# Block 0's V projection: the turned tokens held in TensorE, the weights streamed in 512 columns, and V turned by DMA before its store

## The chip, the cores and the metric

The kernel runs on one core of a Trainium2 chip. The metric is the device time of one execution in microseconds. Three runs of the kernel before gave 1614.95, 1615.28 and 1615.65 us; the median is 1615.28 us. The profile shows one more execution: it took 1615.54 us, and its span, from its first to its last profiled instruction, is 1613.7 us.

## The reference

The input is 2048 tokens of 1024 values in bf16. Two pairs of layers follow each other; each pair is an attention layer and a gated layer, both with a layer norm before and a residual sum behind:

```python
x = A_x
x = x + _A_ref(_layernorm(x, axis=-1), A_wqkv, A_wo)
x = x + _B_ref(_layernorm(x, axis=-1), B_W_gate, B_W_up, B_W_down)
x = x + _A_ref(_layernorm(x, axis=-1), A_wqkv, A_wo)
x = x + _B_ref(_layernorm(x, axis=-1), B_W_gate, B_W_up, B_W_down)
```

`_A_ref` multiplies by `wqkv` (1024 x 3072) and splits the result into q, k and v of 32 heads with 32 values each. A token attends to eight earlier tokens at distances 0, 2, ..., 14; the weighted sum of their v goes through `wo` (1024 x 1024). `_B_ref` computes `relu(x @ W_gate) * (x @ W_up)` with 3584 columns and multiplies by `W_down`.

## The kernel before, in words

The tokens are cut into four blocks of 512 (`BLK`), a block into four tiles of 128 tokens (`TPB`). With two layer pairs there are eight rounds `n`; `n` 0 to 3 are the four blocks of the first pair. All of the change lies in the attention of `n = 0`, in the first 110 us.

A projection needs the normalised tokens with the 1024 channels on the partitions. `xn` holds tokens on partitions, `xnT` holds the turned form, eight chunks `kc` of 128 channels. For blocks 1 to 3 `xn` is turned by a DMA (`turn` in `ln_steps`, L291): tile by tile in block 1, in one transfer of 1 MB in blocks 2 and 3. Block 0 is written by hand in `ln_first` (L327) and `v_first` (L483): tiles 0 to 2 are turned on TensorE (`tp`) and copied back, tile 3 by DMA (`turn_last`). Tiles 0 and 1 are turned before their factor 1/std is known. So `spread_rstd` (L399) lays the factors of these 256 tokens out along the free axis on all partitions (`rb`: four VectorE transposes and six GpSimd copies), and `widen` (L411) multiplies `xnT` of both tiles by it in place, which q and k need.

V of block 0 is needed with channels on partitions, because the scratch tensor `v_d` in HBM is stored channel by channel. The kernel before holds a 128 x 128 piece of the weights in TensorE and streams turned tokens: 192 products of 128 columns and 32 of 256 columns (`prod` in `v_first`). The result in PSUM is V turned already. VectorE evicts tiles 0 and 1 with the factor `rb` (`scaled`), ScalarE evicts tiles 2 and 3. `store_v(0)` writes the whole `vT` to `v_d` in one transfer, and `load_v_steps(0)` reads it back as `vhm`, one transfer per tile, with a halo of 14 tokens.

After V of block 0, TensorE computes q and k of block 0, then q and k of block 1, V of blocks 1, 2 and 3, then q and k of blocks 2 and 3, with eight products of 512 columns per 128 output columns (1.73 us, `GRP`). PSUM gives six banks for these results (tag `acc`). q and k of block 1 are evicted by ScalarE into staging tiles (`qst`, `kst`; pool `stage`, six buffers in a ring) and put to HBM by SyncE's queue (`put`); so `kst` number 7 gets the buffer of `kst` number 1 and has to wait until that one is stored.

What sets the order of the work:

- `ev` is a list of (time, step). It is sorted by the time written there, and the steps are emitted in that order (`emit`).
- TensorE, VectorE and SyncE's DMA queue run in exactly the emitted order: `mm` (L141), `dv` (L115) and `sp_dma` (L130) tie each instruction to the one before it. All DMAs named here go through SyncE's queue, which waits at its head.
- ScalarE and GpSimd are tied only in places (`tail_act`, `last`). Elsewhere the framework's scheduler chooses the order when the program is built, by its own estimate of when each operand is ready. That order is fixed in the program: at run time ScalarE takes its instructions strictly one after the other.
- A buffer that is reused brings a wait for the last reader of what was in it; the pool `early` has three such buffers for `xn` and `vT`.

Of the kernel before, what the change touches and what calls it, by code (L numbers as in the profile page):

```python
# [8 lines left out]
F32 = mybir.dt.float32  # L9
ALU = mybir.AluOpType  # L10
# [3 lines left out]
P = 128  # L14
# [5 lines left out]
HALO = (W - 1) * DIL  # L20
KC = D // P
BLK = 512
TPB = BLK // P
EPS = 1e-5
NEG = -1.0e9
SLAB = 512
# [5 lines left out]
def _ap(t, off, dims):  # L32
    return bass.AP(tensor=t.tensor, offset=t.offset + off, ap=[list(t.ap[0])] + [list(d) for d in dims])
# [3 lines left out]
def kernel(  # L37
# [11 lines left out]
    nc = tc.nc  # L49
# [31 lines left out]
    psum = ctx.enter_context(tc.tile_pool(name="psum", bufs=6, space=bass.MemoryType.PSUM))  # L81
# [28 lines left out]
    def dv(f, *args, **kwargs):  # L110
        if tail_dve[0] is None:
            tail_dve[0] = f(*args, **kwargs).ins
        else:
            with tc.issue_after(tail_dve[0]):
                tail_dve[0] = f(*args, **kwargs).ins  # L115
# [8 lines left out]
    def sp_dma(dst, src, transpose=False):  # L124
        start = nc.sync.dma_start_transpose if transpose else nc.sync.dma_start
        if tail_sp[0] is None:
            tail_sp[0] = start(dst, src).ins
        else:
            with tc.issue_after(tail_sp[0]):
                tail_sp[0] = start(dst, src).ins  # L130

    @contextmanager
    def pe_group():
        if tail_pe[0] is None:
            yield
        else:
            with tc.issue_after(tail_pe[0]):
                yield

    def mm(*args, **kwargs):  # L140
        tail_pe[0] = nc.tensor.matmul(*args, **kwargs).ins  # L141

    def big_tile(shape, name, early=False):
        where = pool["early"] if early else big
        return where.tile(shape, BF16, tag="big", name=name)
# [47 lines left out]
    slab = {}  # L193
# [133 lines left out]
    def ln_first():  # L327
# [4 lines left out]
        def on(eng, f, *args, **kwargs):  # L332
            if eng == "v":
                dv(f, *args, **kwargs)
            elif eng in last:
                with tc.issue_after(last[eng]):
                    last[eng] = f(*args, **kwargs).ins
            else:
                last[eng] = f(*args, **kwargs).ins
# [19 lines left out]
        def power(t, var, sign, eng="g"):  # L359
            vpe = small("vpe1")  # L360
            rstd[t] = pair[:, t:t + 1] if t < 2 else small("rstd1")[:]
            if eng == "v":
                on("v", nc.vector.tensor_scalar, vpe[:], var, EPS, None, op0=ALU.add)
            else:
                on("g", nc.gpsimd.tensor_scalar, vpe[:], var, sign, EPS, op0=ALU.mult, op1=ALU.add)
            on("g", nc.gpsimd.tensor_tensor, rstd[t], vpe[:], neg_half[:, 0:1], op=ALU.pow)
# [27 lines left out]
        def act_power(t, sq):  # L394
            nvar = small("nvar1")
            on("v", nc.vector.scalar_tensor_tensor, nvar[:], mean[t], mean[t], sq[:], op0=ALU.mult, op1=ALU.subtract)
            power(t, nvar[:], -1.0)

        def spread_rstd():  # L399
            rb = hold["rb"] = pool["early"].tile([P, 2, P], F32, tag="rb", name="rb", bufs=1)  # L400
# [41 lines left out]
        def open_up():  # L442
# [5 lines left out]
            for h in range(4):  # L448
# [5 lines left out]
            power(0, square_of(xna[:, 0, :])[:], 1.0)  # L454

        hold.update(on=on, bn=bn, aggr=aggr, apply=apply, turn=turn, copy=copy, widen=widen,
                    spread_rstd=spread_rstd, open_up=open_up, last=last, square_of=square_of, act_mean=act_mean,
                    act_power=act_power)
        return hold

# [21 lines left out]

    def v_first(ln):  # L483
        st = att[0]
        pairs, opened = {}, set()

        def prod(kc, c, t0, t1):
            part = t0 // 2
            if (part, c // 2) not in pairs:
                pairs[part, c // 2] = psum.tile([P, 2, BLK // 2], F32, tag="acc", name="acc_v")  # L490
            acc = pairs[part, c // 2][:, c % 2, (t0 % 2) * P:(t0 % 2 + t1 - t0) * P]
            with pe_group():
                mm(acc, lhsT=slab["v0", kc // (KC // 2)][:, kc % (KC // 2), c * P:(c + 1) * P],
                   rhs=ln["xnT"][:, t0:t1, kc, :], start=(part, c // 2) not in opened, stop=(kc == KC - 1),
                   skip_group_check=True)
            opened.add((part, c // 2))

        def scaled(i):
            dv(nc.vector.tensor_tensor, st["vT"][:, 2 * i:2 * i + 2, 0:2 * P], pairs[0, i][:],
               _ap(ln["rb"], 0, [[0, 2], [1, 2 * P]]), op=ALU.mult)  # L500

        def later(t, h):
            ln["turn"](t, (h,))
            ln["copy"](t, "a", h, 2 - h)

        def turn_last():
            sp_dma(ln["xnT"][:, TPB - 1, :, :], ln["xn"][:, TPB - 1, :], True)
            load_x(1, [1])

        def halves(i, part, k0):  # L510
            for c in (2 * i, 2 * i + 1):
                for kc in range(k0, KC):
                    prod(kc, c, 2 * part, 2 * part + 2)

        def head():
            st["vT"] = big_tile([P, KC, BLK], "vT_0", True)
            ln["open_up"]()

            def chunk(kc, t):
                for c in range(KC):  # L520
                    prod(kc, c, t, t + 1)

            for kc in range(3):
                chunk(kc, 0)
            ln["turn"](1, (0,))
            ln["copy"](1, "v", 0)
            ln["turn"](1, (1,))
            ln["copy"](1, "a", 1)
            chunk(3, 0)
            ln["spread_rstd"]()  # L530
            for kc in range(4):
                chunk(kc, 1)
            for c in range(KC):
                prod(4, c, 0, 2)
            ln["bn"](2, 0)
            ln["bn"](2, 1)
            ln["aggr"](2)
            sq = ln["square_of"](x_tiles[3][:])
            ln["act_mean"](3)
            ln["act_power"](3, sq)  # L540
            ln["apply"](2)
            ln["apply"](3)
            turn_last()
            for c in range(KC):
                prod(5, c, 0, 2)
            for c in range(4):
                prod(6, c, 0, 2)
            for i in range(KC // 2):
                if i == 3:
                    later(2, 0)  # L550
                halves(i, 0, 7 if i < 2 else 6)
                if i == 3:
                    later(2, 1)
                scaled(i)
            ln["widen"]()
            q = KC // 4
            for cs, kcs in ((range(0, 2 * q), range(0, q)), (range(0, 2 * q), range(q, 2 * q)),
                            (range(2 * q, 3 * q), range(0, 2 * q)), (range(0, 2 * q), range(2 * q, KC)),
                            (range(3 * q, KC), range(0, 2 * q)), (range(2 * q, KC), range(2 * q, KC))):
                for c in cs:  # L560
                    for kc in kcs:
                        prod(kc, c, 2, 3)
            for c in range(KC):
                for kc in range(KC):
                    prod(kc, c, 3, 4)
                if c % 2 == 1:
                    ln["on"]("a", nc.scalar.copy, st["vT"][:, c - 1:c + 1, 2 * P:BLK], pairs[1, c // 2][:])
            tail_act[0] = ln["last"]["a"]

        return head  # L570

    def store_v(n):
        def f():
            dst = bass.AP(tensor=v_d.tensor, offset=v_d.offset + HALO + (n % NB) * BLK,
                          ap=[[NTOK, P], [P * NTOK, KC], [1, BLK]])
            sp_dma(dst, att[n]["vT"][:])
        return f
# [202 lines left out]
    def load_v_steps(n):  # L780
        b = n % NB

        def f_(tq):
            def f():
                if tq == 0:
                    att[n]["v_hm"] = soft.tile([P, DH, HALO + P], BF16, tag="v_hm", name=f"vhm_{n}")
                src = bass.AP(tensor=v_d.tensor, offset=v_d.offset + b * BLK + tq * P,
                              ap=[[DH * NTOK, H], [NTOK, DH], [1, HALO + P]])
                sp_dma(att[n]["v_hm"][32 * tq:32 * tq + 32, :, :], src)
            return f  # L790

        return [f_(tq) for tq in range(TPB)]
# [188 lines left out]
    def spread(steps, at, gap):  # L981
        for i, f in enumerate(steps):
            ev.append((at + gap * i, f))
# [54 lines left out]
               (t_sum0 - 0.1, t_sum0 + 4.5, t_sum0 + 4.6), (t_qk0 + 10.6, t_qk0 + 15.8, t_qk0 + 15.9)]  # L1038
    for t, steps in enumerate(norm_at):
        ev.extend(zip(steps, (stats[t], apply[t], turn(t))))  # L1040
    ev.append((t_qk0 + 4.0, store_v(0)))
    ev.append((t_qk0 + 18.0, lambda: load_x(3)))
    spread(qk_steps(0, ln_a[0], "qk01"), t_qk0, GRP)
    spread(prod_sum_steps(0), t_sum0, 4.4)
    spread(load_v_steps(0), t_qk0 + 19.0, 1.0)
    ln1(2, t_qk0 + 17.5, t_qk1 + 17.0, True, 4.5)
    qk1, puts1, gets1 = (part[0::2] + part[1::2] for part in qk_steps(1, ln_a[1], "qk01", True))
    spread(qk1, t_qk1, GRP)
# [142 lines left out]
```

## Time and profile before

| what | value |
|---|---|
| median of the runs | 1615.28 us (1614.95 to 1615.65) |
| the profiled execution, its span | 1615.54 us, 1613.7 us |
| TensorE busy | 1606.9 us, all 40 slices at 9 tenths or more, granted clock 1.00 |
| waits of TensorE in the whole span | 1.1 us and 0.4 us, both before 7.5 us |
| VectorE, ScalarE, GpSimd busy | 1139.4, 477.5, 186.7 us |
| V of block 0 on TensorE | 5.8 to 21.8 us, 224 products and 16 turns |
| V of blocks 1 to 3 on TensorE | 76.9 to 119.0 us |
| ScalarE busy from 42 to 76 us | nearly all of it |

Times in the views are microseconds from the start of the span. A busy TensorE is not by itself TensorE at its peak, since ends of products are modelled; how many products run in a stretch says more. A row of the timeline gives start, duration, engine, line, operation, tiles, shape and count; neighbours of the same kind are merged into one row. Durations of SyncE's rows are the time that issuing takes; the time to landing stands in the DMA view.

### The profile page before, as it was taken

Reading aid. Unit: us, or ns where it says so; the run is one execution under the profiler, and the core shown is the slowest. Engines: PE = TensorE matmul, PEld = TensorE weight load, DVE = VectorE, ACT = ScalarE, POOL = GpSimd, SP = SyncE. Lnnn points to the kernel's source line nnn. Section 1 sums busy time; section 2 is a strip of 40 time slices with the busy share of each in tenths; the row PEclk is TensorE's granted clock in tenths of the full one; section 3 lists DMA queues with packets and bytes.
Section 4 is the critical chain, followed back from the end, with each engine's and each line's share of the span. In section 5 each row is a group of like instructions: output and inputs, shape, how many; then the busy total and the mean of one; then the engine's idle time right before and its main releaser. Section 6 shows DMA issues by size and latency. Waiting matters only on the chain.

```text
span 1613.7 us, 18950 instructions
## 1 busy us (share of the span) xinstructions
PE 1606.9 (100%) x7604; PEld 785.4 (49%) x7653; DVE 1139.4 (71%) x963; ACT 477.5 (30%) x978; POOL 186.7 (12%) x173
## 2 busy tenths in 40 slices
PE   9999999999999999999999999999999999999999
PEld 7646544444444445444454444544445444444444
DVE  6999978997989698929389393993939939311211
ACT  4953311131115313603136031361313311131110
POOL 3400000010003002300053000530005100000000
PEclk9999999999999999999999999999999999999999
DMA  9977867596669666784747857488574874655452
GB/s 285 201 202 251 211 173 244 185 227 203 200 199 230 190 187 200 202 244 147 228 154 206 233 158 227 155 197 257 164 227 155 207 241 157 209 160 179 157 165 71
DMA packets 360473, 318.20 MB, mean 197 GB/s; under 512 B 106304, under 2 KB 334656, under 8 KB 359872
## 3 DMA queue, kind: packets, MB, share of 16 engines
q1 hardware_dynamic: 359808, 316.36, 67.1%
q8 instruction: 60, 0.98, 0.3%
q10 hardware_dynamic: 576, 0.62, 0.1%
q14 instruction: 29, 0.24, 0.1%
HBM read 266.29 MB, written 34.66 MB: 186 GB/s over the span
## 4 chain that ended last, share of the span: by engine, by line
PE 86%; DVE 10%; DMA 2%; issue 1%; ACT 0%; SPq 0%; POOL 0%; DVEq 0%; ACTq 0%; POOLq 0%
PE acc_u L141 21%; PE acc_g L141 21%; PE dacc L141 17%; PE acc_v L141 6%; PE dacc_pair L141 6%; PE acc_wo L141 5%; PE acc_q L141 5%; PE acc_k L141 5%; DVE pv L115 4%; DVE ac L115 2%; DVE t L115 2%; DMA s<-s_d 1%; DVE hT L115 1%; DVE x L115 0%; DMA xnT_b<-xn_b 0%
## 5 line engine op out<-in xcount | busy, mean ns | idle before, releaser
L141 PE MATMUL acc_g<-xnT_b,w_g 128*128 128x512 bf16 x1792 | 423.3, 379 | 0.0
L141 PE MATMUL acc_u<-xnT_b,w_u 128*128 128x512 bf16 x1792 | 423.3, 379 | 0.0
L891 ACT ACTIVATE r<-acc_g 128x512 bf16<-128x512 f32 x224 | 133.6, 596 | 721.2 <-PE acc_g L141 678.0
L115 DVE TENSOR_TENSOR hT<-acc_u,r 128x512 bf16<-128x512 f32 x224 | 150.8, 686 | 240.2 <-PE acc_u L141 237.6
L141 PE MATMUL dacc<-w_d,hT 128*128 128x512 bf16 (+1 forms) x1372 | 301.9, 376 | 1.5
L141 PEld LDWEIGHTS <-hT 128*128 128x128 bf16 x1820 | 177.0, 98 | 210.2
L141 PEld LDWEIGHTS <-w_u 128*128 128x128 bf16 x1792 | 175.4, 98 | 211.4
L141 PEld LDWEIGHTS <-w_g 128*128 128x128 bf16 x1792 | 175.3, 98 | 211.4
L115 DVE TENSOR_TENSOR pv<-a,vhm 128x4096 bf16<-128x4096 bf16 x64 | 143.5, 2283 | 0.0
L943 DVE TENSOR_TENSOR x<-dacc,x 128x512 bf16<-128x512 f32 (+1 forms) x38 | 24.7, 676 | 154.0 <-PE dacc L141 154.0
L704 DVE TENSOR_TENSOR t<-q,k 128x2048 f32<-128x2048 bf16 x56 | 128.0, 2292 | 6.7 <-ACT k L640 4.6
L115 DVE TENSOR_TENSOR t<-q,k 128x2048 f32<-128x2048 bf16 x56 | 127.3, 2284 | 0.9
L645 POOL COPY kh<-k 128x14 bf16<-128x14 bf16 x40 | 58.4, 1467 | 497.9 <-ACT k L640 497.9
L115 DVE TENSOR_TENSOR pv<-pv 128x1024 bf16<-128x1024 bf16 (+1 forms) x128 | 113.7, 949 | 0.0
L141 PE MATMUL acc_wo<-w_o,oT 128*128 128x512 bf16 x498 | 111.1, 379 | 0.7
L720 DVE TENSOR_TENSOR ac<-ac,t 128x2048 f32<-128x2048 f32 x48 | 109.7, 2285 | 0.3
L115 DVE TENSOR_TENSOR ac<-ac,t 128x2048 f32<-128x2048 f32 x48 | 109.6, 2283 | 0.0
L274 POOL TENSOR_TENSOR st_b<-st_b,neg_half 128x1 f32<-128x1 f32 x29 | 45.8, 1586 | 526.4 <-ACT st_b L273 521.6
L141 PE MATMUL dacc_pair<-w_d,hT 128*128 128x512 bf16 (+1 forms) x413 | 94.0, 375 | 0.4
L141 PEld LDWEIGHTS <-oT 128*128 128x128 bf16 x512 | 50.1, 98 | 60.4
L269 ACT ACTIVATE xn_b<-x 128x1024 bf16<-128x1024 bf16 x29 | 30.3, 1045 | 132.8 <-DVE x L115 70.6
L478 ACT CAST vT<-acc_v 128x512 bf16<-128x512 f32 x56 | 32.5, 585 | 54.3 <-PE acc_v L141 53.3
(142 smaller groups left out, 1235.3 us busy)
## 6 DMA issues: line engine op xcount, KB each, us to landing
w_g<-in_B_W_gate_dram SPq DMA_DIRECT2D x56, 1024.0 KB, 7.1
w_u<-in_B_W_up_dram SPq DMA_DIRECT2D x56, 1024.0 KB, 5.3
w_d<-in_B_W_down_dram SPq DMA_DIRECT2D x48, 1024.0 KB, 5.8
w_o<-in_A_wo_dram SPq DMA_DIRECT2D x16, 1024.0 KB, 8.3
vhm<-v_d SPq DMA_DIRECT2D x32, 284.0 KB, 6.8
v_d<-vT SPq DMA_DIRECT2D x8, 1024.0 KB, 9.5
oT<-o_d SPq DMA_DIRECT2D x32, 256.0 KB, 3.6
w_d<-in_B_W_down_dram SPq DMA_DIRECT2D x16, 512.0 KB, 3.6
```

What stands on the lines that cost most here:

```text
L115: tail_dve[0] = f(*args, **kwargs).ins
L141: tail_pe[0] = nc.tensor.matmul(*args, **kwargs).ins
L269: nc.scalar.activation(xn, xt[:], ACT.Square, accum_out=sq)
L274: nc.gpsimd.tensor_tensor(rstd, vpe, neg_half[:, 0:1], op=ALU.pow)
L478: tail_act[0] = nc.scalar.copy(st["vT"][:, c, :], acc[:]).ins
L645: nc.gpsimd.tensor_copy(khalo[n][:, c, :], k[:, BLK:BLK + HALO])
L704: nc.vector.tensor_tensor(t[:], i0, i1, op=ALU.mult)
L720: nc.vector.tensor_tensor(o, i0, i1, op=ALU.add)
L891: tail_act[0] = nc.scalar.activation(rs[j][:], acc[:], ACT.Relu).ins
L943: run = dv if n < NB - 2 else (lambda f, *args, **kwargs: f(*args, **kwargs))
```

## The change

Block 0's V is computed the other way round: a 128 x 128 piece of the turned tokens is held, and 512 columns of the weights stream past it. That makes 64 products instead of 224, and V comes out with tokens on partitions. It is evicted into `xn` of block 0, whose contents are no longer needed: tiles 0 and 1 by VectorE with the factor 1/std as a value per partition (`rpair`), tiles 2 and 3 by ScalarE (`put` in `v_first`). `spread_rstd` is called later, the small steps around tile 3's factor are ordered differently, and one of them goes from GpSimd to VectorE.

Because V is now not turned, four DMA turns on SyncE's queue (`turn_v`) bring it into `vT` after block 3's tokens have been requested. Five transfers store it to `v_d` (`store_v_first`), written at times between the puts of block 1's q. `load_v_steps(0)` moves from `t_qk0 + 19.0` to `t_qk1 + 17.1`, just behind the turn of block 2.

```diff
-        def act_power(t, sq): ...  power(t, nvar[:], -1.0)
+        def act_power(t, sq): ...  power(t, nvar[:], -1.0, "v")
...
-                mm(acc, lhsT=slab["v0", kc // (KC // 2)][:, kc % (KC // 2), c * P:(c + 1) * P],
-                   rhs=ln["xnT"][:, t0:t1, kc, :], start=(part, c // 2) not in opened, stop=(kc == KC - 1),
-                   skip_group_check=True)
...
-        def scaled(i):
-            dv(nc.vector.tensor_tensor, st["vT"][:, 2 * i:2 * i + 2, 0:2 * P], pairs[0, i][:],
-               _ap(ln["rb"], 0, [[0, 2], [1, 2 * P]]), op=ALU.mult)
+        def prod(kc, t):
+            for h in range(2):
+                if kc == 0:
+                    accs[t, h] = psum.tile([P, SLAB], F32, tag="acc", name="acc_v")
+                with pe_group():
+                    mm(accs[t, h][:], lhsT=ln["xnT"][:, t, kc, :],
+                       rhs=slab["v0", kc // (KC // 2)][:, kc % (KC // 2), h * SLAB:(h + 1) * SLAB],
+                       start=(kc == 0), stop=(kc == KC - 1))
+
+        def put(t):
+            for h in range(2):
+                v = ln["xn"][:, t, h * SLAB:(h + 1) * SLAB]
+                if t < 2:
+                    dv(nc.vector.tensor_scalar, v, accs.pop((t, h))[:], ln["rpair"][:, t:t + 1], None, op0=ALU.mult)
+                else:
+                    ln["on"]("a", nc.scalar.copy, v, accs.pop((t, h))[:])
...
-            chunk(3, 0)
-            ln["spread_rstd"]()
...
+            ln["apply"](2)
             ln["act_power"](3, sq)
-            ln["apply"](2)
             ln["apply"](3)
             turn_last()
...
+            ln["spread_rstd"]()
+            prod(6, 0)
+            prod(7, 0)
+            put(0)
+            later(2, 0)
+            prod(6, 1)
+            later(2, 1)
+            prod(7, 1)
+            put(1)
             ln["widen"]()
+            for t in range(2, TPB):
+                for kc in range(KC):
+                    prod(kc, t)
+                put(t)
...
+    def turn_v(t):
+        def f():
+            if t == 0:
+                att[0]["vT"] = big_tile([P, KC, BLK], "vT_0", True)
+            sp_dma(att[0]["vT"][:, :, t * P:(t + 1) * P], ln_a[0]["xn"][:, t, :], True)
+        return f
+
+    def store_v_first(c0, c1):
+        def f():
+            dst = bass.AP(tensor=v_d.tensor, offset=v_d.offset + HALO + c0 * P * NTOK,
+                          ap=[[NTOK, P], [P * NTOK, c1 - c0], [1, BLK]])
+            sp_dma(dst, att[0]["vT"][:, c0:c1, :])
+        return f
...
-    ev.append((t_qk0 + 4.0, store_v(0)))
+    spread([turn_v(t) for t in range(TPB)], t_qk0 + 19.0, 0.01)
+    spread([store_v_first(c0, c1) for c0, c1 in ((0, 2), (2, 4), (4, 6), (6, 7), (7, 8))], t_qk1 + 3.4, 0.87)
...
-    spread(load_v_steps(0), t_qk0 + 19.0, 1.0)
+    spread(load_v_steps(0), t_qk1 + 17.1, 0.01)
```

More of the change, by code (lines that the diff above doesn't have):

```diff
@@ L362, in power @@
             if eng == "v":
-                on("v", nc.vector.tensor_scalar, vpe[:], var, EPS, None, op0=ALU.add)
+                on("v", nc.vector.tensor_scalar, vpe[:], var, sign, EPS, op0=ALU.mult, op1=ALU.add)
             else:
@@ L396, in act_power @@
             on("v", nc.vector.scalar_tensor_tensor, nvar[:], mean[t], mean[t], sq[:], op0=ALU.mult, op1=ALU.subtract)
-            power(t, nvar[:], -1.0)
+            power(t, nvar[:], -1.0, "v")
         def spread_rstd():
@@ L456, in ln_first @@
         hold.update(on=on, bn=bn, aggr=aggr, apply=apply, turn=turn, copy=copy, widen=widen,
-                    spread_rstd=spread_rstd, open_up=open_up, last=last, square_of=square_of, act_mean=act_mean,
+                    rpair=pair, spread_rstd=spread_rstd, open_up=open_up, last=last, square_of=square_of, act_mean=act_mean,
                     act_power=act_power)
@@ L484, in v_first @@
         st = att[0]
[L485 to L492, printed above, removed]
-                mm(acc, lhsT=slab["v0", kc // (KC // 2)][:, kc % (KC // 2), c * P:(c + 1) * P],
-                   rhs=ln["xnT"][:, t0:t1, kc, :], start=(part, c // 2) not in opened, stop=(kc == KC - 1),
-                   skip_group_check=True)
-            opened.add((part, c // 2))
-        def scaled(i):
-            dv(nc.vector.tensor_tensor, st["vT"][:, 2 * i:2 * i + 2, 0:2 * P], pairs[0, i][:],
-               _ap(ln["rb"], 0, [[0, 2], [1, 2 * P]]), op=ALU.mult)
+        accs = {}
+        def prod(kc, t):
[13 more added lines that the diff above has]
+                    ln["on"]("a", nc.scalar.copy, v, accs.pop((t, h))[:])
         def later(t, h):
@@ L508, in turn_last @@
             load_x(1, [1])
[L510 to L513, printed above, removed]
         def head():
-            st["vT"] = big_tile([P, KC, BLK], "vT_0", True)
             ln["open_up"]()
-            def chunk(kc, t):
-                for c in range(KC):
-                    prod(kc, c, t, t + 1)
             for kc in range(3):
-                chunk(kc, 0)
+                prod(kc, 0)
             ln["turn"](1, (0,))
@@ L528, in head @@
             ln["copy"](1, "a", 1)
-            chunk(3, 0)
-            ln["spread_rstd"]()
+            prod(3, 0)
             for kc in range(4):
-                chunk(kc, 1)
-            for c in range(KC):
-                prod(4, c, 0, 2)
+                prod(kc, 1)
+            for kc in range(4, 6):
+                for t in range(2):
+                    prod(kc, t)
             ln["bn"](2, 0)
@@ L539, in head @@
             ln["act_mean"](3)
+            ln["apply"](2)
             ln["act_power"](3, sq)
-            ln["apply"](2)
             ln["apply"](3)
             turn_last()
[L544 to L554, printed above, removed]
-            ln["widen"]()
[L556 to L563, printed above, removed]
+            ln["spread_rstd"]()
[7 more added lines that the diff above has]
+            put(1)
+            ln["widen"]()
+            for t in range(2, TPB):
                 for kc in range(KC):
-                    prod(kc, c, 3, 4)
-                if c % 2 == 1:
-                    ln["on"]("a", nc.scalar.copy, st["vT"][:, c - 1:c + 1, 2 * P:BLK], pairs[1, c // 2][:])
+                    prod(kc, t)
+                put(t)
             tail_act[0] = ln["last"]["a"]
         return head
+    def turn_v(t):
[10 more added lines that the diff above has]
+        return f
     def store_v(n):
```

## The prediction

> **What bounds the kernel now.** I read the page's busy times first, then TensorE's waits, then its timeline, which together say whether a wait added anywhere can hide.
>
> ```profile
> PE 1606.9 (100%) x7604; PEld 785.4 (49%) x7653; DVE 1139.4 (71%) x963; ACT 477.5 (30%) x978; POOL 186.7 (12%) x173
> ...
> PE scratch L141 <- DVE ones L319: 1.1, 1, 1.1
> PE acc_v L141 <- DMA w_v<-in_A_wqkv_dram: 0.4, 1, 0.4
> ```
>
> ```profile
> 8.50 5.29 PE acc_v L141 x68
> 14.68 7.15 PE acc_v L141 x128
> 21.83 5.19 PE acc_q L141 x24
> 63.28 13.81 PE acc_k L141 x64
> 77.09 24.17 PE acc_v L141 x112
> ```
>
> The first fence is the page's busy line and all of TensorE's waits (in all, times, longest), the second holds pieces of the chain in order of time (start, length, what). 64 products of 512 columns take 13.81 us, 215.8 ns each. From 21.83 us to the last product's end at 1611.11 (the chain's end) are 1589.3 us. The program has 7360 such products there (gate and up 3584, down 1792, wo 512, q and k 1024, V 448), 1588.3 us, plus 0.6 for the eight `L` products. So TensorE streams without a gap: it is the bound everywhere, and a microsecond of waiting put in anywhere lengthens the kernel by one.
>
> The next views are timelines (start, length, engine, what) of ScalarE, SyncE and TensorE, and between the last two the DMA view of 92 to 104 us (how many, us to landing).
>
> ```profile
> 82.41 0.57 ACT L637 CAST kst<-acc_k 128x512 bf16<-128x512 f32 x1
> 83.08 1.05 ACT L478 CAST vT<-acc_v 128x512 bf16<-128x512 f32 x2
> ...
> 101.30 0.58 ACT L478 CAST vT<-acc_v 128x512 bf16<-128x512 f32 x1 [1.14 <-PE acc_v L141]
> ```
>
> ```profile
> 46.60 5.18 SPq L130 DMA_DIRECT2D vhm<-v_d  x4
> 72.41 6.59 SPq L130 DMA_TRANSPOSE xnT_a<-xn_a  x1
> 79.05 4.37 SPq L130 DMA_DIRECT2D k_d<-kst  x6
> 84.61 0.46 SPq L130 DMA_DIRECT2D k_d<-kst  x1
> 93.02 4.92 SPq L130 DMA_TRANSPOSE xnT_a<-xn_a  x1
> ```
>
> ```profile
> xnT_a<-xn_a SPq DMA_TRANSPOSE x1, 6.8
> ```
>
> ```profile
> 119.02 27.79 PE L141 MATMUL acc_q<-xnT_a,w_qk_q 128*128 128x512 bf16 x128
> ```
>
> The last `kst` is cast at 82.41 and put at 84.61; block 3's turn is issued at 93.02 and lands 6.8 us later, at 99.8 (the DMA view of that stretch). V of block 3 ends where `acc_q` starts, 119.02, so its 64 products start at 119.02 - 13.81 = 105.21. The turn has 5.4 us to spare.
>
> **The change, part by part.**
>
> 1. *V's products.* Before: 40 of 128 columns at 7.15/128 = 55.9 ns take 2.24 us of the 5.29 us piece, so the 28 of 256 columns in it take 109 ns each. TensorE waits for weights at 7.4 us in both, so only work after that counts: 176 x 55.9 ns + 32 x 109 ns = 13.33 us. After: 60 x 215.8 ns = 12.95. Gain 0.38 us. One load of a held operand takes 98 ns (page), under 215.8, so it stays covered.
>
> 2. *The rest of the head.* Evictions: four on VectorE for four (2.46 us together before), four casts on ScalarE for four. `spread_rstd` (1.04 us of VectorE, 1.78 of GpSimd) moves behind `apply(3)`. From VectorE's rows (tile 2's statistics at 9.77 at the latest, as before, then `apply(2)` to 12.7, `apply(3)` to 14.3, spread 1.04, evictions 2.46, `widen` 2.34) `widen` ends near 20.2; q starts at 21.66 - 0.38 = 21.28. Cost nothing, cover 1.1 us; beyond that, us for us. Tile 2's turns on TensorE come at about 13.2, after `apply(2)`. The turn of tile 3 is issued about 14.3 instead of 14.57 and lands 3.2 us later, before tile 3's products at 18.
>
> 3. *Four turns and five stores.* The turns follow block 3's token loads (46.5) and, because `vT` takes the buffer of block 1's `xn`, the landing of that block's last turn (about 48.7: issue 42.7 plus the median 6.0). Four issues at 1.3 us end near 54; they land near 56 (1 MB at the 217 GB/s of the 93 us turn is 4.8 us; three issues and 3.2 to landing, 7.0). They stand where the four `vhm` loads stood, whose DMA work lasted to 57. Then the stores (1 MB) go out among the puts of `qst`: put 0 as before, put 1 some 3 us later than at 54.6, put 2 one or two. ScalarE needs put 1's landing at 65.5 and put 2's at 66.6, and six PSUM banks (10 us) stand behind it. The DMA engines are nearly idle from 58 to 66. Cost nothing; upper end, if turns and stores each land 3 us later than said: 2 us. The one store removed at 34.5 frees 0.6 us of the queue, which then waits for ScalarE's 42.7 anyway.
>
> 4. *`vhm` behind block 2's turn.* Its readers start at 110 us, so the load itself is on time. But its four issues (5.18 us in all) now stand ahead of the puts of `kst` 1 to 6, which go from 79.05 to about 84.3 and land behind 1.1 MB of short rows (some 7 us of DMA before): 88 to 91. `kst` 7 needs `kst` 1's buffer, so its cast cannot run at 82.41. The built program has drawn the consequence already: the scheduler moved that cast. ScalarE's fixed order around it:
>
> ```
> before: ... kst 6, (layer norm), kst 7, V1 casts 0..7, V2 casts 0..5, V2 cast 6 ...
> after:  ... kst 6, (layer norm), V1 casts 0..7, V2 casts 0..5, kst 7, V2 cast 6 ...
> ```
>
> The bank of `acc_k` 7 stays occupied meanwhile; the built program gives V five banks, whose casts keep up (they wait for products in the rows above). That costs nothing. But SyncE's order is unchanged: put of `kst` 7, *then* block 3's turn, then the stores of V1 and V2 and the loads of block 1's q and k. So the turn now waits for a cast 19 us later:
>    - V2's cast 5 starts at 101.30 - 0.38 = 100.92, one cast of a pair takes 0.47 (1.05 for two, 0.58 for one), so `kst` 7 runs from 101.39 to 101.97;
>    - its put issues in 0.46: 102.45;
>    - the turn lands 6.8 us later: 109.25. DMA is idle then, as at 93 us (0.12 of a share at 102 to 104 before).
>    - V of block 3 could start at 105.21 - 0.38 = 104.83. **Stall 4.4 us.**
>
>    Lower end: 1 MB moves in 4.8 us at 217 GB/s with nothing around it, landing 107.25, stall 2.4. Upper: block 2's turn took 8.8, stall 6.4. I take 6.8, the same transfer at the same size under an idle DMA.
>
> 5. *Behind the stall.* Loads of block 1's q and k move from 106.7 to about 108.5; their products on VectorE start at 144.19. The store of `o` and the loads of `oT` (144 to 149) go at most 4 us later, like their reader `wo` at 157. VectorE's softmax starts from `L` at 101.2, before the stall, and later waits for TensorE as now. Nothing more.
>
> Sum: -0.38 + 4.4 = **+4.0 us**. The profiled execution took 1615.54 (span 1613.7 plus 1.8 around it), so 1619.6; the median of the runs shown lies 0.26 lower, so **1619.3**. Step 1's gain alone cannot be told from no change: 0.2%, 3.2 us, is about what a measurement of this kernel tells from none.
>
> **Rivals.**
>
> - *The stall cools TensorE's clock.* The kernel's first nine `scratch` products take 4.02 us, 447 ns each, and then the rate doubles: a half-speed state exists after idling. If 4.4 us of waiting brings it back, nine products cost 4.02 instead of 1.94: +2.1 us, 1621.4. For it: the wait is as long as that slow stretch. Against: no wait within this trace is longer than 1.1 us, so nothing shows it happening in mid-run. [...]
> - *No stall; not slower.* The turn of block 3 is ready in time, and only -0.38 remains: 1614.9. The place is SyncE's put of `kst` 7; it decides at 98.0, since a turn issued before 104.83 - 6.8 costs nothing. For it: 5.4 us of slack before, and idle DMA. Against: the built order puts six V2 casts ahead, and the sixth cannot run before TensorE's product at 100.9.
> - *A second stall in the staging ring.* If the V turns and stores delay the puts of q by more than the banks cover (step 3) or `oT` misses its 157 (step 5), some 2 to 4 us more: 1621 to 1624. Against: covers of 6 us and more.
> - *Clearly faster* would need 3.2 us of waiting in TensorE to be taken away; there are 1.5, all at the start. Its chance is for something unseen.
>
> **Chances.** The 4.4 us stall at full clock 0.53; with a cooled clock 0.20; a second stall 0.07; no stall 0.16; faster 0.04. The likeliest gives 1619.3, with its own range 1617.5 to 1621.5 from step 4's ends. The whole range takes in the cooled clock and part of the second stall, and leaves out the cases without a stall: 1617.0 to 1623.5. Slower by over 0.2% begins at 1618.5: 0.92 of the first case, the second and third, together 0.76; same 0.16 + 0.04 = 0.20; faster 0.04.
>
> **What the profile after would show.** Step 1: V of block 0 in 64 products, q starting near 21.3. Step 2: no wait of `acc_q` there. Step 4: the last `kst` cast at about 101.4, block 3's turn issued at about 102.5, and a new wait of TensorE, `acc_v` for `xnT_a`, of 4 us at about 105 to 109. Clock: products at about 447 ns behind it, or a granted clock below 1.00 in that window, if it cools. Step 3: no wait between 49 and 77. I am wrong if no such wait stands there, if the turn is issued near 93, or if `wo` at 157 waits.

## The result, and the profile after

The changed kernel takes 1621.05 us (median, 1620.63 to 1621.83), beside 1615.43 us of the kernel before (1614.89 to 1615.74) on the same chip. The ratio is 1.0036, with a 95% interval of 1.0023 to 1.0049: 5.6 us slower, inside the predicted range, in the predicted direction, and 1.75 us above the predicted time. The profiled execution took 1621.83 us, the longest of them, with a span of 1620.1 us (before 1613.7): 6.4 us to account for.

TensorE's waits in the whole span of the changed kernel (in all, times, longest):

```profile
PE acc_v L141 <- DMA xnT_a<-xn_a: 4.3, 1, 4.3
PE scratch L141 <- DVE ones L319: 1.1, 1, 1.1
PE acc_v L141 <- DMA w_v<-in_A_wqkv_dram: 0.2, 1, 0.2
```

One wait is new, and it is the forecast one: V of block 3 for block 3's turn. No other wait has come. The chain of the same execution (start, length, what) runs through that turn:

```profile
101.00 1.02 PE acc_v L141 x5
102.03 6.78 DMA xnT_a<-xn_a
108.81 0.05 issue
108.86 16.71 PE acc_v L141 x64
125.56 4.53 PE acc_q L141 x21
```

Two things stand in it. The chain (followed back from the last instruction, at each step to what released it) leaves TensorE at 102.03 for the transfer and comes back at 108.81. And the 64 products behind it take 16.71 us, where the same 64 take 13.81 us elsewhere: something slows them as well.

Why the turn was late is read on SyncE's queue and on ScalarE (timelines of the changed kernel):

```profile
46.76 5.40 SPq L130 DMA_TRANSPOSE vT<-xn_first  x4
...
71.23 5.31 SPq L130 DMA_TRANSPOSE xnT_a<-xn_a  x1
76.59 3.78 SPq L130 DMA_DIRECT2D vhm<-v_d  x4
80.41 4.16 SPq L130 DMA_DIRECT2D k_d<-kst  x6
...
101.59 0.34 SPq L130 DMA_DIRECT2D k_d<-kst  x1
102.03 4.83 SPq L130 DMA_TRANSPOSE xnT_a<-xn_a  x1
```

```profile
100.50 0.59 ACT L478 CAST vT<-acc_v 128x512 bf16<-128x512 f32 x1 [1.14 <-PE acc_v L141]
100.98 0.59 ACT L632 CAST kst<-acc_k 128x512 bf16<-128x512 f32 x1
```

The last `kst` is cast at 100.98 instead of 82.41, since ScalarE's built order has it behind six of block 2's V casts, the sixth of which waits for its products. The buffer that it needs was free some 10 us sooner: the six puts of `kst` ahead were issued by 84.57 and landed at most 6.3 us later. So the larger part of the delay comes from the order fixed when the program was built. SyncE's put of that `kst` therefore goes out at 101.59 instead of 84.61, and block 3's turn, which stands right behind it in that queue, at 102.03 instead of 93.02.

TensorE's rows give the price:

```profile
100.94 3.63 PE L141 MATMUL acc_v<-xnT_a,w_v 128*128 128x512 bf16 x16
108.86 16.71 PE L141 MATMUL acc_v<-xnT_a,w_v 128*128 128x512 bf16 x64 [4.29 <-DMA xnT_a<-xn_a]
125.40 4.91 PE L141 MATMUL acc_q<-xnT_a,w_qk_q 128*128 128x512 bf16 x22
```

Sixteen products from 100.94 would have let V of block 3 start at 104.39 (16 x 215.8 ns); it started at 108.86, 4.47 us late. From there to `acc_q` are 16.54 us instead of 13.81, 2.73 us more. And q of block 0 began 0.79 us earlier in the head (20.87, before 21.66). Together 4.47 + 2.73 - 0.79 = 6.41 us, which is the whole difference of the spans. The profile's clock row by stretches names the 2.73: the granted clock is 0.50 from 107.6 to 114.4 us. Its lines are shown with the experiments on it.

### The profile page after: what moved, and what is told of

It is laid out like the page before. It is cut to its first block, busy times and chain, and to the rows that moved or that the text cites. A ratio compares the mean times of both kernels' runs of the same rounds, so it can differ in the third digit from the quotient of the medians.

```text
span 1620.1 us, 18642 instructions
## 1 busy us (share of the span) xinstructions
PE 1609.1 (99%) x7443; PEld 777.8 (48%) x7493; DVE 1140.6 (70%) x964; ACT 477.8 (29%) x978; POOL 183.9 (11%) x172
## 4 chain that ended last, share of the span: by engine, by line
PE 99%; DMA 1%; issue 0%; SPq 0%; DVE 0%
PE acc_g L141 24%; PE acc_u L141 24%; PE dacc L141 18%; PE acc_q L141 7%; PE acc_k L141 7%; PE acc_v L141 7%; PE acc_wo L141 7%; PE dacc_pair L141 5%; DMA xnT_a<-xn_a 0%; DMA w_v<-in_A_wqkv_dram 0%; PE tp L432 0%; SPq L130 0%; PE L L141 0%; SPq L127 0%; DVE x L938 0%
## 5 line engine op out<-in xcount | busy, mean ns | idle before, releaser
L640 POOL COPY kh<-k 128x14 bf16<-128x14 bf16 x40 | 53.0, 1332 | 497.2 <-ACT k L635 497.1
```

The costliest lines, as they stand in the source:

```text
L640: nc.gpsimd.tensor_copy(khalo[n][:, c, :], k[:, BLK:BLK + HALO])
```

## The experiments

The kernel before took 1615.28 us (1614.95 to 1615.82) beside e1 to e4, 1615.26 us (1614.89 to 1615.74) beside e5 to e7, and 1615.38 us beside e8 and e9.

### e1: the last put of `kst` behind block 3's turn

```diff
-    spread(puts1, t_qk1 + GRP + 1.2, GRP)
+    spread(puts1[:-1], t_qk1 + GRP + 1.2, GRP)
+    ev.append((t_v2 + 0.5, puts1[-1]))
```

> The changed kernel with one step moved: the put of kst 7 is emitted behind block 3's turn instead of ahead of it. The cast of kst 7 stays where the scheduler has it, behind six casts of V2, and the vhm loads stay ahead of the puts of kst 1 to 6. Theory (SyncE's queue waits at its head for that cast): the turn is issued near 92, lands near 99, no wait of TensorE at 104, no slow clock; 1614.5 to 1615.2. Rival (the turn is late because the vhm loads and V's stores crowd the DMA engines, or because the layer norm of block 3 is late on ScalarE): the wait stays, near 1621.

Measured: 1615.34 us (1615.1 to 1615.6), ratio 1.0000, interval 0.9991 to 1.0010. The cast of that `kst` is as late as in the changed kernel (101.12) and its put goes out at 101.74, but the turn is issued at 92.36, ahead of it, and what is left of V of block 2 runs into V of block 3 as one row of 80 products without a wait. SyncE's and TensorE's rows of e1:

```profile
92.36 4.83 SPq L130 DMA_TRANSPOSE xnT_a<-xn_a  x1
101.74 0.36 SPq L130 DMA_DIRECT2D k_d<-kst  x1
```

```profile
101.08 17.44 PE L141 MATMUL acc_v<-xnT_a,w_v 128*128 128x512 bf16 x80
```

So it is the place in SyncE's queue, behind that put, that costs the 5.6 us. With the turn ahead of the put, the later cast, the new V products, the turns and the stores together leave the time where it was before.

It also brought a surprise: not 1614.5 to 1615.2, as expected from the early start of q, but no gain at all. TensorE's rows of e1 show where the gain goes:

```profile
170.16 7.07 PE L141 MATMUL acc_k<-xnT_a,w_qk_k 128*128 128x512 bf16 x32
177.52 10.52 PE L141 MATMUL acc_k<-xnT_a,w_qk_k 128*128 128x512 bf16 x48 [0.30 <-DVE x L115]
```

32 products from 170.16 end at 177.07; the next starts at 177.52, 0.45 us late, waiting for VectorE to empty a bank of the output projection.

### e2: the reload of V behind block 1's V products

```diff
-    spread(load_v_steps(0), t_qk1 + 17.1, 0.01)
+    spread(load_v_steps(0), t_v1 + 3.0, 0.01)
```

> The changed kernel with the four vhm loads moved behind the puts of kst 1 to 7, just ahead of block 3's turn. In the built program the cast of kst 7 is back ahead of V1's first cast. Theory (the place of the vhm loads is what made the scheduler move the cast): no wait of TensorE at 104, 1614.5 to 1615.2. Rival (the four turns of V and their stores are what delays block 3's turn): wait and time stay near 1621.

Measured: 1615.31 us (1615.12 to 1615.47), ratio 1.0000, interval 0.9991 to 1.0009. Here the cause is taken away one step earlier: SyncE puts the six `kst` at 76.67, ahead of the reload at 81.47, ScalarE's order has the last `kst` cast first again, and block 3's turn goes out at 92.28. SyncE's rows of e2:

```profile
76.67 3.02 SPq L130 DMA_DIRECT2D k_d<-kst  x6
81.47 8.37 SPq L130 DMA_DIRECT2D vhm<-v_d  x4
92.28 5.39 SPq L130 DMA_TRANSPOSE xnT_a<-xn_a  x1
```

Again there is no stall at 104 us, and the same wait of 0.30 us, ending at 177.46. Both ways of freeing the turn give the same time, so nothing else in the change costs more than the head gains.

### e3: TensorE kept busy during the wait

```diff
+    ev.append((t_v3 - 0.01, lambda: scratch(20)))
```

Twenty dead products of the block of ones run ahead of V of block 3; the stall stays.

> The changed kernel with 20 products of 512 columns put ahead of V of block 3, into a PSUM bank that nobody reads: 20 x 215.8 ns = 4.3 us of work inside the 4.3 us wait. Theory (the wait lets TensorE's clock fall to half, and that costs the 2.9 us by which the 64 products behind it took longer than 13.81): the turn lands as late as before, but the granted clock stays 1.00 and the time falls by 2.9 to about 1618.1. Rival (the clock falls for another reason, for instance what the DMA engines or VectorE do at that time, or the products of the new form before it): clock 0.50 behind the wait, 1621 or more.

Measured: 1619.39 us (1619.04 to 1619.9), ratio 1.0026, interval 1.0016 to 1.0035, granted clock 1.00 throughout. TensorE's rows:

```profile
104.74 4.48 PE L141 MATMUL scratch<-ones 128*128 128x512 bf16 x20
109.18 13.99 PE L141 MATMUL acc_v<-xnT_a,w_v 128*128 128x512 bf16 x64
123.01 7.29 PE L141 MATMUL acc_q<-xnT_a,w_qk_q 128*128 128x512 bf16 x33
```

V of block 3 starts as late as before (109.18), but takes 13.83 us to `acc_q`, its normal time. So the change costs 4.1 us by the late turn (less the head's gain) and, by the medians, 1.7 us (1621.05 less 1619.39) by what idling does to the clock. The time is not the expected 1618.1, because the 2.9 us was read in the longest execution (2.73 us by its rows) and taken off the median; most executions of the changed kernel had less to win back. It is idling and not the turn's own traffic that slows the products, for the same transfer is in flight here.

### e4: only the reload moved, in the kernel before

```diff
-    spread(load_v_steps(0), t_qk0 + 19.0, 1.0)
+    spread(load_v_steps(0), t_qk1 + 17.1, 0.01)
```

Everything else is the kernel before, with its old V products and its one store.

> The kernel before with one line of the change: the vhm loads moved behind block 2's turn. V's products, eviction and store are as before. Theory: the same built order (kst 7 behind six casts of V2), the same wait of 4.4 us and the same slow clock, without the head's gain: 1615.4 + 4.4 + 2.9 = 1622, between 1621 and 1623. Rival (the wait needs the four turns or the new products): 1615.4.

Measured: 1622.25 us (1621.47 to 1622.77), ratio 1.0043, interval 1.0028 to 1.0058, with the same new wait of `acc_v` for `xnT_a`, 4.3 us. TensorE's rows:

```profile
109.33 16.79 PE L141 MATMUL acc_v<-xnT_a,w_v 128*128 128x512 bf16 x64 [4.31 <-DMA xnT_a<-xn_a]
125.95 4.26 PE L141 MATMUL acc_q<-xnT_a,w_qk_q 128*128 128x512 bf16 x19
```

One moved line makes the whole loss; the new form of V is not needed for it. The time is 1.2 us above the changed kernel's. e4 lacks the head's gain, and its clock lost more: the mean granted clock that each execution has on record is 0.998 in three of e4's four executions, but in two of the changed kernel's six, and 0.999 in the others.

### e5: e2 with GpSimd's old order

What took the head's gain in e1 and e2? VectorE's additions were late because the layer norm on it waited for GpSimd. GpSimd's and then VectorE's rows of the kernel before:

```profile
170.76 0.55 POOL L311 TENSOR_TENSOR rstd<-vpe,neg_half 128x1 f32<-128x1 f32 x1 [86.53 <-DVE vpe L115]
171.85 0.55 POOL L274 TENSOR_TENSOR st_b<-st_b,neg_half 128x1 f32<-128x1 f32 x1 [0.54 <-ACT st_b L273]
```

```profile
171.34 0.55 DVE L115 TENSOR_SCALAR xn_b<-x,mv,rstd 128x1024 bf16<-128x1024 bf16 x1 [0.66 <-POOL rstd L311]
```

And the same of e1:

```profile
171.19 0.55 POOL L274 TENSOR_TENSOR st_b<-st_b,neg_half 128x1 f32<-128x1 f32 x1 [87.20 <-ACT st_b L273]
171.71 0.55 POOL L311 TENSOR_TENSOR rstd<-vpe,neg_half 128x1 f32<-128x1 f32 x1
```

```profile
172.29 0.55 DVE L115 TENSOR_SCALAR xn_b<-x,mv,rstd 128x1024 bf16<-128x1024 bf16 x1 [2.27 <-POOL rstd L311]
```

GpSimd runs its instructions in the built order. In the kernel before, tile 1's `rstd` stands ahead of tile 0's `st_b`; in the changed kernel and in e1 and e2 the scheduler has swapped the two, at 171 us, far behind the edit. e4 has them swapped too, so the moved reload is enough for it. So `rstd`, ready at 170 us, waits for `st_b`, whose input comes from ScalarE at 171. e5 is e2 with the old order tied down (the step of tile 0 is emitted behind those of tile 1, and its GpSimd instruction is tied behind theirs):

```diff
-                if t == 0:
+                if "st" not in hold:
...
-                nc.gpsimd.tensor_tensor(rstd, vpe, neg_half[:, 0:1], op=ALU.pow)
+                with (tc.issue_after(pow_dve[0]) if dve and not early else nullcontext()):
+                    nc.gpsimd.tensor_tensor(rstd, vpe, neg_half[:, 0:1], op=ALU.pow)
...
-        nc.gpsimd.tensor_tensor(rstd[:], vpe[:], neg_half[:, 0:1], op=ALU.pow)
+        pow_dve[0] = nc.gpsimd.tensor_tensor(rstd[:], vpe[:], neg_half[:, 0:1], op=ALU.pow).ins
...
-    ln2(0, wo_ats, 3.0, ...
+    ln2(0, [wo_ats[0] + 0.05] + wo_ats[1:], 3.0, ...
```

> The run with the reload behind block 1's V products, and one change more: on GpSimd, the reciprocal root of block 0's tile 1 (rstd, whose mean and variance VectorE has ready first) stands again ahead of that of tile 0 (st_b), as in the kernel before. Theory: the early start of 0.7 us was not lost by itself but in this queue: VectorE waited 2.27 us for rstd there, instead of 0.66, its additions of the output projection came late, and TensorE waited 0.30 us at 177.5 us for a bank. With the old order VectorE waits some 0.7 us again, TensorE's wait at 177.5 us is gone, the gate and up products start at about 187.4 us instead of 187.88, and the time is about 1614.85 us, 0.45 under that of the run before it. Rival: the gain is taken back further on, because other work sets when the gate and up products or the end can come: then the wait at 177.5 us goes, but the time stays at 1615.3 us.

Measured: 1614.70 us (1614.51 to 1615.09). GpSimd's `rstd` runs at 169.99 and VectorE waits 0.67 us for it. TensorE's rows have no wait there any more:

```profile
170.06 17.43 PE L141 MATMUL acc_k<-xnT_a,w_qk_k 128*128 128x512 bf16 x80
187.33 1.89 PE L141 MATMUL acc_g<-xnT_b,w_g 128*128 128x512 bf16 x8
```

The gate and up products start at 187.33 (187.82 in e2, 188.09 before), and the span is 1613.0 us (e2 1613.5, before 1613.7). So the swapped pair was what took the gain. The traces leave nothing else: by operations and tiles, e5's order differs from e2's in this pair alone, on every engine (on TensorE by its weight loads) and in SyncE's queue, and behind 90 us this pair is also the only difference of order between the kernel before and e2. e5 is the shortest of all these kernels, 0.56 us under the kernel before by medians; its ratio is 0.9997 with an interval of 0.9989 to 1.0006, so the times alone do not exclude that the two are equal.

### e6 and e7: half and a quarter of the wait covered

e3 with ten, and with five, dead products instead of twenty.

> The changed kernel with 10 dead products of the block of ones (the scratch products of the head, 0.216 us each, 2.2 us) ahead of block 3's V products, instead of the 20 that kept the clock. TensorE is then idle for only about 2.2 us before block 3's V products. Theory: the clock falls only after about 3 us without a product (2.9 us after the last product's end in the changed kernel, 3.2 us in the kernel before with only the reload moved), so it stays at 1.00 here, block 3's 64 V products take 13.9 us, and the time is that with 20 dead products, 1619.4 us. Rival: what counts is the mean load over a longer stretch and not one empty one: then the clock falls here too for part of the time, and the time lies between 1619.4 and 1621.1 us.

> The same with 5 dead products (1.1 us): TensorE is idle for about 3.2 us, close to what it took for the clock to fall in the two runs where it fell. Theory: if the clock looks at stretches that start at times of their own, it falls in some executions and not in others, and for a shorter part of the wait: the times spread between 1619.4 and 1621.1 us, and the median is near 1620. Rival: the clock follows the length of the idle time with a fixed bound: all executions then agree, at 1619.4 us (bound above 3.2 us) or at 1621.0 us (bound below it).

Measured, e6: 1619.3 us (1618.97 to 1621.12), ratio 1.0027, interval 1.0016 to 1.0038. In the profiled execution TensorE idles 2.1 us, and V of block 3 takes 13.82 us, its time at full clock. (The view's 1.00 says nothing here: this trace holds no record of the clock, and the view prints 1.00 where there is none.) Six of its seven executions lie between 1618.97 and 1619.41, with a mean granted clock of 1.000; the one at 1621.12 has 0.999.

Measured, e7: 1621.15 us, and a wider spread than expected: 1619.08, 1621.01, 1621.30 and 1622.28, with mean granted clocks of 1.000, 0.999, 0.999 and 0.998; ratio 1.0036, interval 1.0022 to 1.0050. TensorE's rows of the profiled one:

```profile
104.69 1.24 PE L141 MATMUL scratch<-ones 128*128 128x512 bf16 x5
109.12 16.90 PE L141 MATMUL acc_v<-xnT_a,w_v 128*128 128x512 bf16 x64 [3.19 <-DMA xnT_a<-xn_a]
125.86 4.48 PE L141 MATMUL acc_q<-xnT_a,w_qk_q 128*128 128x512 bf16 x20
```

So these runs show no fixed bound on the idle time: executions of one program, which waits 3.19 us in the profiled one, are 3.2 us apart. The clock fell in this execution 2.3 us after the last dead product had ended (105.93 to 108.23), sooner than the 3 us that I had taken for the bound. By the mean clocks it fell in one of seven executions with some 2.1 us of idling and in three of four with some 3.2 us; with 4.3 us no execution of the changed kernel or of e4 took less than 1620.3 us. In all twelve of those executions (eight of the changed kernel with e8 and e9, four of e4) the mean granted clock is below 1.000. When in an execution the clock fell, and how long TensorE idled there, is known only of the profiled ones.

### e8 and e9: the changed kernel's clock in two more executions

No edit.

> The changed kernel once more, for a second record of the clock. In the records so far the slow stretch lasted 6.8 to 6.95 us and cost block 3's V products 2.9 us, but the changed kernel's times (1620.63 to 1621.83 us) lie only 1.2 to 2.5 us above those with the clock kept, 1619.35. Theory: the slow stretch begins at a time of the clock's own and lasts 6.8 us always; it can begin no sooner than some 2 us after the last product at 104.6, so at 106.6 or later, and 4.5 us or more of it lie on products that begin at 108.9: a loss of 2.2 us or more, 1621.6 us or more. Rival: the slow stretch is shorter in some executions, such as 3.4 us: then a time between 1620.6 and 1621.2 us goes with a stretch of about 3 us at half clock, and 1.2 to 1.7 us lost.

> The same kernel again, for a third record, with the same expectations: by the theory 1621.6 us or more and 6.8 us at half clock, by the rival a time in step with a slow stretch that is shorter in this execution or in the one before.

Measured: 1621.23 and 1620.33 us, both under the 1621.6 us of the theory. The clock in windows of 0.1 us, at the two edges of the slow stretch (window, core us, busy TensorE, weight loads, VectorE, ScalarE, GpSimd, granted clock, DMA share, GB/s). The changed kernel's first profile:

```profile
107.50:107.60 0.10, 0.00 (x0) 0.00 (x0) 0.10 (x1) 0.00 (x0) 0.00 (x0) 0.88 1.19 223
...
114.40:114.50 0.10, 0.10 (x2) 0.09 (x1) 0.10 (x1) 0.00 (x0) 0.00 (x0) 0.98 1.42 256
```

e8:

```profile
110.10:110.20 0.10, 0.10 (x3) 0.04 (x1) 0.10 (x1) 0.00 (x0) 0.00 (x0) 0.83 1.10 389
...
113.50:113.60 0.10, 0.10 (x2) 0.05 (x1) 0.10 (x1) 0.00 (x0) 0.00 (x0) 0.60 1.14 225
```

e9:

```profile
108.10:108.20 0.10, 0.00 (x0) 0.00 (x0) 0.10 (x1) 0.00 (x0) 0.00 (x0) 0.64 1.15 384
...
111.50:111.60 0.10, 0.10 (x1) 0.00 (x0) 0.10 (x1) 0.00 (x0) 0.00 (x0) 0.80 1.05 277
```

A window that straddles an edge gives the edge itself, since the clock is 1.00 on one side and 0.50 on the other: 0.88 means 0.076 us at 1.00, so the fall is at 107.58. The loss is the time from V of block 3 to `acc_q` less 13.81 us.

| execution | fall | return | length | V of block 3 from | loss | half of the slow time with products |
|---|---|---|---|---|---|---|
| changed kernel, first | 107.58 | 114.40 | 6.83 | 108.86 | 2.73 | 2.77 |
| e8 | 110.17 | 113.58 | 3.41 | 109.29 | 1.70 | 1.71 |
| e9 | 108.13 | 111.54 | 3.41 | 108.70 | 1.40 | 1.42 |
| e4 | 108.20 | 115.03 | 6.83 | 109.33 | 2.81 | 2.85 |
| e7 | 108.23 | 115.06 | 6.83 | 109.12 | 2.93 | 2.97 |

My theory of a constant 6.8 us fell: the slow stretch is 3.41 us in two of the five records and 6.83 us in three, and the loss is half of its part with products, to 0.05 us in each of the five. In four of them the clock fell before the products began again, 2.30 us (e7), 3.01 us (the first profile), 3.18 us (e4) and 3.70 us (e9) after the last product's end. In e8 it stayed up through the whole wait of 4.27 us and fell 0.88 us after the products had begun again. What decides when the clock falls and when it returns was not shown.

## Why the prediction was right or wrong

- **The bound.** Right. TensorE streams everywhere, and the stall and the slow clock went to the end in full: 4.47 + 2.73 - 0.79 us is the difference of the two spans.
- **Step 1, 0.38 us.** The sum was about right. With the old form q of block 0 starts at 21.66 (before) and 21.31 (e4), with the new one at 20.73 to 21.32 in nine records, 21.04 on the mean: 0.4 us earlier. In single executions two waits move it by as much: that for the weights at 7 us (0.44 us in the profile before, 0.16 after, none in e4), and one of the first turns for VectorE (0.89 us in e8, none in the profiles before and after). So the 0.79 us between the two profiles is in part luck.
- **Step 2.** Right: no wait of `acc_q`; `widen` ends at 19.9 (20.2 said).
- **Step 3.** Right: the four turns are issued by 52.2 (54 said), and there is no wait between 49 and 77. The cover was thinner than "nearly idle": the DMA share of the kernel before is 0.69 from 60 to 62 us and 0.35 from 62 to 64.
- **Step 4.** Right in its mechanism, and in the stall to the tenth: the cast at 100.98 (101.39 said), the turn issued at 102.03 (102.45) and landed 6.78 us later (6.8), the stall 4.47 us (4.4). e1 and e2 take it away from either side, and e4 makes it with the one moved line alone.
- **Step 5.** Right: no further wait behind the stall.
- **The clock: the step that failed.** I gave "full clock" 0.53 and the rival "the stall cools TensorE's clock" 0.20, and the rival is what happened, in all three records of the changed kernel; the mean granted clock is below 1.000 in its five other executions too. The time lies in the range because the range took in this rival; the likeliest value, 1619.3 us, missed by 1.75 us, which is about what the clock cost. "Against: no wait within this trace is longer than 1.1 us" was only an absence of evidence: a trace without a long wait can say nothing of one. The 0.20 was an estimate that no run stood behind. The price, 2.1 us, was near the middle of what was measured (1.4, 1.7 and 2.7 us in the records, 1.7 by the medians), but not for its reason: nine slow products would lose 1.9 us, since they start 427 ns apart (the 4.02 us of their row hold the end of the last one too), and in the records the loss is half of the slow stretch's part with products (1.42 and 1.71 us where it lasted 3.41 us, 2.77 where it lasted 6.83), not the price of nine products. Had the rival been the forecast, 1621.4 us, it would have been 0.35 us off.
- **The rival "No stall", 1614.9 us.** It did not happen, and when e1 and e2 made it happen the time was 1615.3. What the prediction left out is GpSimd's built order behind the head: the swap of `rstd` and `st_b` at 171 us. The changed kernel has it too, and there it costs nothing, because TensorE is late anyway. Without the swap (e5) the time is 1614.7.

## What to carry to other kernels

Where a queue runs strictly in order, look for the slowest producer behind *each* entry ahead of the one that matters: here four loads cost nothing themselves, but delayed a put, the put a buffer, the buffer a cast (most of it in the order that the scheduler built), the cast a second put, and that one the transfer that TensorE needed. A new wait of TensorE can cost more than its own length: here the five profiled executions with a wait of 3.19 to 4.31 us and a slow stretch lost another 1.40 to 2.93 us to the clock, the three of the changed kernel among them 1.40, 1.70 and 2.73 us. And after an edit, compare the built order of *every* engine to its end, since one pair that the scheduler swapped at 171 us took back most of a gain made at 21 us.

## What the runs showed that I had not expected

- The clock did not fall at one length of idle time: in e7 it fell 2.3 us after the last product, and in e8 0.9 us after products had resumed, with 4.27 us of waiting behind it. It came back after 3.41 us in e8 and e9, and after 6.83 us in the first profile, e4 and e7.
- Dead products were a cheap cover for the clock here: ten of them (2.2 us) in a wait of 4.3 us saved 1.75 us by the medians (1621.05 to 1619.3), as much as twenty, though one of seven executions lost the clock all the same. They did nothing for the wait itself: V of block 3 starts at 109.17 us with them and at 108.86 without.
- TensorE runs at half rate when the kernel starts, though the view prints a granted clock of 1.00 there: the trace has no record before the clock's first rise, at 5.18 us in the changed kernel and 6.08 in the kernel before. The nine `scratch` products start 427 ns apart instead of 215.8, and the products of 128 columns behind them go from 107 to 56 ns apart at just these two times.
